# First loads of an attention and two-MoE kernel in another order, one weight tile decoded in halves

## The chip, the cores and the metric

The kernel runs on one core of a Trainium2 chip. The metric is device time in microseconds (us) of one execution; 1 us is 0.07% of it.

## The reference

Eight batches of eight heads attend, over 576 positions, to 32 memory slots that are built from the keys and values; two feed-forward layers follow. Cut to what matters:

```python
a = softmax(phi, axis=2)                                  # over the 32 slots
k_m, v_m = a^T @ k, a^T @ v                               # einsum bhsm,bhsd->bhmd
attn = softmax(q @ k_m^T / sqrt(64))
x = (attn @ v_m), heads side by side: [4608, 512]
x = (silu(x @ w_gate) * (x @ w_val)) @ w_out              # d_ff 1536
out = elu(x @ w_in) @ w_out2                              # d_ff 2048
```

The weights come as 64-bit floats, everything else as 32-bit.

## The kernel before

The heads' outputs are never formed. For each batch the 32 slots' values (vt, 128 partitions) are multiplied with the gate and value weights first, into vw (the product pvw, L237), and the softmaxed scores (at) are multiplied with vw (up1, L255 to L257). Each product that needs 32-bit accuracy is made of three fast ones: both sides are split into a high and a low part, and high x high, high x low and low x high are added.

The weights of the first layer lie in HBM as words of eight bytes. `words` and `load_w` (L119 to L144) decode a tile: one conversion on ScalarE (L126), then five steps on VectorE (L127, L128, L130, L131, L144). `load_wg(p, k2, pool, parts)` decodes tile k2 of pair p; pair p holds the weights for two of the hidden layer's blocks of 128 and comes as two tiles (k2 = 0, 1) of 1 MB. With `parts=2` a tile is decoded in two halves, ten steps of 128x512 for five of 128x1024. Tiles of pair 0 of the code are called **pair 1** here and in the change's description, those of `w1g[1, k2]` **pair 2**, with tile 0 (`raw[1, 0]`) and tile 1 (`raw[1, 1]`).

The stage around the change is the start (L506 to L534), for batch 0. ScalarE and VectorE softmax phi; TensorE transposes it (a_T, L347) and multiplies it with five chunks of keys and values (kv_mm, L364), the fifth of half size; the result is scaled (L371), transposed (L377) and copied to kT and vt (L380 to L388). Scores of the first half of the positions (L411) are transposed by VectorE (L416), reduced to a maximum (L422), subtracted (L423), passed through exp on ScalarE (L424), summed and divided (L429 to L432), and transposed back as ex (L451); ScalarE and VectorE split that into the high and low part of at (L453, L454). The second half's scores (L400, L402) go the same way in another layout. pvw of pair 1 (`vw(0, 0, G2)`) gives the first gate and value products; pvw of pair 2 comes inside the loop over batches, after a filler of 13 products that nobody reads (`spin`, L300). Copies of vw are ScalarE's L246 and L248, with a product by minus one (L247) between them. The output weights w1o are decoded there as well (`load_wo`; its split into woh is L171).

What sets the order: the loads are issued by SP in the order of the code. Each takes one of eight semaphores in turn, so a load is issued once the one eight before it has landed. The order of the instructions on TensorE, VectorE and ScalarE is made when the program is built, by a scheduler that starts what its own estimate of the times says is ready, `tc.high_priority()` first. On the chip each engine's list is fixed.

Of the kernel before, what the change touches and what calls it, by code (L numbers as in the profile page):

```python
# [27 lines left out]
NCH = 5  # L28
# [10 lines left out]
def attention_moe_moe(ctx: ExitStack, tc: tile.TileContext, qT, phiT, kv, kv4, w1g, w1o, w2, out):  # L39
# [5 lines left out]
    w1g, w1o, w2 = w1g.bitcast(I32), w1o.bitcast(I32), w2.bitcast(I32)  # L45

    dram = ctx.enter_context(tc.tile_pool(name="dram", bufs=1, space=DRAM))
    wa_p = ctx.enter_context(tc.tile_pool(name="wa", bufs=NWA))
# [53 lines left out]
    def fetch_part(r, src, i, parts=2):  # L102
        n = 1024 // parts
        cs = slice(n * i, n * i + n)
        nc.sync.dma_start(out=r[:, cs], in_=src[:, 2 * n * i:2 * n * i + 2 * n].rearrange("p (n t) -> p n t", t=2))
# [5 lines left out]
    def fetch_w(src):  # L111
        r = raw_tile()
        fetch_part(r, src, 0, 1)
        return r
# [26 lines left out]
    def load_w(v, r):  # L141
        with later():
            cf = words(v, r)
            last["sum"] = tt(out=v, in0=v, in1=cf, op=ALU.add)  # L144
# [4 lines left out]
    def load_wg(p, k2, pool, parts=1):  # L149
        t = pool.tile([128, 2, 512], F32, tag="w", name="wg")  # L150
        WG[p][2 * k2], WG[p][2 * k2 + 1] = t[:, 0], t[:, 1]
        r = raw.pop((p, k2), None)
        if r is None:
            r = fetch_w(w1g[p, k2])
        t = t.rearrange("p i c -> p (i c)")
        n = 1024 // parts
        for i in range(parts):
            cs = slice(n * i, n * i + n)
            load_w(t[:, cs], r[:, cs])
        ahead((p, k2))  # L160
# [30 lines left out]
    def ahead(key):  # L191
        if key in ORDER[:-1]:
            fetch_next(ORDER.index(key) + 1)
# [32 lines left out]
    raw = {}  # L226
# [248 lines left out]
    def back_tasks(b):  # L475
        z, nxt = Bs[b], Bs[b + 1] if 0 < b < B - 1 else None
        yield lambda: z.score(0)
        yield lambda: (z.norm(0), nxt and nxt.load_q(0))
        yield lambda: (z.attn(0))
        yield lambda: (z.score(1), 0 < b < B - 2 and Bs[b + 2].phi())  # L480
        yield lambda: (z.norm(1), nxt and nxt.load_q(1))
        yield lambda: (z.attn(1), z.store_at())
# [7 lines left out]
    def run(*gens):  # L490
        for g in gens:
            for t in g:
                t()
# [11 lines left out]
    z = Bs[0]  # L505
# [4 lines left out]
    z.load_kv(0)  # L510
    z.load_kv(1)
    fetch_part(raw[0, 1], w1g[0, 1], 0)
    for c in range(2, NCH):
        z.load_kv(c)
    fetch_part(raw[0, 1], w1g[0, 1], 1)
    z.load_q(0)
    for k2 in range(2):
        raw[1, k2] = vx_p.tile([128, 1024, 2], I32, tag="vx", name="wr1")
        fetch_part(raw[1, k2], w1g[1, k2], 0, 1)
        if k2 == 0:  # L520
            z.load_q(1)
    b0 = list(back_tasks(0))
    with tc.high_priority():
        z.phi()
# [3 lines left out]
    vw(0, 0, G2)  # L528
    first["ex"] = last["ex"]
    for k2 in range(2):  # L530
        load_wg(1, k2, wa_p)
    run(b0[3:])
    first["ex"] = last["ex"]
    load(Bs[1])  # L534
# [577 lines left out]
```

## Time and profile before

| | |
|---|---|
| median of 3 runs | 1433.72 us (1433.63 to 1433.94) |
| profiled execution, own time | 1434.55 us |
| its span in the trace | 1432.8 us |
| busy: TensorE, VectorE, ScalarE | 1405.6, 1141.7, 857.7 us |
| moved by DMA | 337.65 MB, mean 236 GB/s |
| mean granted clock of TensorE | 0.994 of full |

The span is what the trace covers; the execution's own time has 1.75 us around it. In the rows below a time is counted from the span's start. A duration of one instruction on VectorE or ScalarE overlaps the next one's start a little. A granted clock of 1.00 is 2.4 GHz, one of 0.50 is 1.2 GHz. SP's rows are issues of loads: the row is the issue, not the transfer.

### The profile page before, as it was taken

To read this page: it belongs to the slowest core of one execution; us is meant where nothing else is said; L and a number is where in the kernel's file an instruction comes from. 1 tells how busy PE (TensorE), PEld (TensorE's weight loads), DVE (VectorE), ACT (ScalarE), POOL (GpSimd) and SP (SyncE) were. 2 spreads that over 40 slices of the span, in tenths; PEclk is the share of its full clock that TensorE was granted. 3 is DMA by queue.
4 is the path that set the end of the run, shared out by engine and by line. 5 is a ranking of instruction groups with operands and counts; after the bars stand their busy time and mean duration, and the time that the engine had idled before them with its cause. 6 is when DMAs were issued, how large, how long until landed. Compare 5 with 4: busy or idle time off the path is not lost.

```text
span 1432.8 us, 23223 instructions
## 1 busy us (share of the span) xinstructions
PE 1405.6 (98%) x9269; PEld 1214.2 (85%) x9269; DVE 1141.7 (80%) x1462; ACT 857.7 (60%) x1251; POOL 44.8 (3%) x73
## 2 busy tenths in 40 slices
PE   6899999999999999999999999999999999999998
PEld 4688889998999999999998888888888888888887
DVE  7998887778798886886978578885898488957884
ACT  4665544544456465455656388556866588549843
POOL 0000000000000000000000000000000000000000
PEclk8999999999999999999999999999999999999999
DMA  9887512663789988888889866756675667666653
GB/s 375 321 315 283 195 74 101 224 226 140 265 246 291 297 237 255 258 243 270 282 272 364 282 198 213 273 205 197 205 275 210 199 205 254 224 206 204 214 199 131
DMA packets 89484, 337.65 MB, mean 236 GB/s; under 512 B 9376, under 2 KB 23712, under 8 KB 70048
## 3 DMA queue, kind: packets, MB, share of 16 engines
q1 hardware_dynamic: 55312, 254.04, 50.8%
q10 hardware_dynamic: 26880, 51.39, 9.7%
q0 software_dynamic: 7184, 30.74, 8.9%
q8 instruction: 73, 1.20, 0.3%
q14 instruction: 35, 0.29, 0.1%
HBM read 251.13 MB, written 85.00 MB: 235 GB/s over the span
## 4 chain that ended last, share of the span: by engine, by line
PE 90%; DVE 4%; DMA 3%; issue 1%; ACT 1%; SPq 0%; ACTq 0%; DVEq 0%
PE pu L834 12%; PE pu L832 12%; PE pu L833 12%; PE pd L834 5%; PE pd L832 5%; PE pd L833 5%; PE acc L262 4%; PE acc L260 4%; PE acc L261 4%; PE pv L255 3%; PE pg L255 3%; PE pv L257 3%; PE pv L256 3%; PE pg L257 3%; PE pg L256 3%; PE pvw L237 3%
## 5 line engine op out<-in xcount | busy, mean ns | idle before, releaser
L834 PE MATMUL pu<-xhi,w 128*128 128x512 f32 x672 | 261.4, 389 | 0.0
L833 PE MATMUL pu<-xlo,w 128*128 128x512 f32 x672 | 261.4, 389 | 0.0
L832 PE MATMUL pu<-xhi,w 128*128 128x512 f32 x672 | 261.4, 389 | 0.0
L861 ACT ACTIVATE xhi<-g 128x1024 fp32r<-128x1024 f32 x120 | 126.5, 1058 | 107.0 <-PE pu L834 64.5
L862 DVE TENSOR_TENSOR xlo<-g,xhi 128x1024 fp32r<-128x1024 f32 x120 | 145.3, 1223 | 40.7 <-ACT xhi L861 40.6
L833 PEld LDWEIGHTS pu<-xlo,w 128*128 128x128 f32 x672 | 126.1, 188 | 26.4
L834 PEld LDWEIGHTS pu<-xhi,w 128*128 128x128 f32 x672 | 126.1, 188 | 26.3
L832 PEld LDWEIGHTS pu<-xhi,w 128*128 128x128 f32 x672 | 126.1, 188 | 26.0
L261 PE MATMUL acc<-hh,ws 128*128 128x288 f32 x448 | 131.7, 296 | 0.0
L260 PE MATMUL acc<-hh,ws 128*128 128x288 f32 x448 | 131.5, 295 | 0.0
L262 PE MATMUL acc<-hl,ws 128*128 128x288 f32 x448 | 128.8, 297 | 0.0
L255 PE MATMUL pv<-at,vw 128*128 128x288 f32 x384 | 116.5, 303 | 1.9 <-DVE s L280 1.2
L255 PE MATMUL pg<-at,vw 128*128 128x288 f32 x384 | 116.7, 304 | 0.6 <-DVE gh L658 0.3
L722 ACT ACTIVATE hh<-gh 128x576 fp32r<-128x576 f32 x112 | 76.0, 685 | 67.8 <-PE acc L261 51.3
L256 PE MATMUL pg<-at,vw 128*128 128x288 f32 x384 | 114.0, 297 | 0.2 <-DVE at L454 0.2
L257 PE MATMUL pv<-at,vw 128*128 128x288 f32 x384 | 113.9, 297 | 0.0
L257 PE MATMUL pg<-at,vw 128*128 128x288 f32 x384 | 113.8, 297 | 0.1
L256 PE MATMUL pv<-at,vw 128*128 128x288 f32 x384 | 113.8, 296 | 0.0
L832 PE MATMUL pd<-xhi,w 128*128 128x512 f32 x288 | 112.0, 389 | 0.0
L833 PE MATMUL pd<-xlo,w 128*128 128x512 f32 x288 | 112.0, 389 | 0.0
L834 PE MATMUL pd<-xhi,w 128*128 128x512 f32 x288 | 112.0, 389 | 0.0
L852 DVE SCALAR_TENSOR_TENSOR et<-et 128x1024 f32<-128x1024 f32 x72 | 88.0, 1222 | 28.8 <-ACT et L851 28.8
(155 smaller groups left out, 3239.1 us busy)
## 6 DMA issues: line engine op xcount, KB each, us to landing
w<-dnd SPq DMA_DIRECT2D x64, 1024.0 KB, 4.9
w<-upd SPq DMA_DIRECT2D x40, 1024.0 KB, 5.6
w<-upd SPq DMA_DIRECT2D x32, 768.0 KB, 4.7
ws<-d1d SPq DMA_DIRECT2D x42, 512.0 KB, 5.1
kvr<-kv SPq DMA_DIRECT2D x32, 512.0 KB, 8.9
wr<-w SPq DMA_DIRECT2D x16, 1024.0 KB, 6.5
upd<-uw ACTq DMA_DIRECT2D x32, 512.0 KB, 7.1
dnd<-uw ACTq DMA_DIRECT2D x32, 512.0 KB, 8.2
```

Source lines behind the costliest of these rows:

```text
L255: mm(ps, lhsT=wh, rhs=ah, start=g == 0, stop=False)
L256: mm(ps, lhsT=wh, rhs=al, start=False, stop=False)
L257: last["pe"] = mm(ps, lhsT=wl, rhs=ah, start=False, stop=g == 1)
L260: mm(ps, lhsT=w[0][:, ms], rhs=hs[0], start=start, stop=False, skip_group_check=skip)
L261: mm(ps, lhsT=w[1][:, ms], rhs=hs[0], start=False, stop=False, skip_group_check=skip)
L262: mm(ps, lhsT=w[0][:, ms], rhs=hs[1], start=False, stop=stop, skip_group_check=skip)
L832: mm(ps, lhsT=w[0], rhs=x[0], start=start, stop=False, skip_group_check=skip)
L833: mm(ps, lhsT=w[0], rhs=x[1], start=False, stop=False, skip_group_check=skip)
L834: last["mm"] = mm(ps, lhsT=w[1], rhs=x[0], start=False, stop=stop, skip_group_check=skip)
L852: stt(out=a, in0=e, scalar=1.0, in1=a, op0=ALU.add, op1=ALU.mult)
L861: last["hi"] = act(out=hi, in_=x, func=AF.Copy)
L862: last["lo"] = tt(out=lo, in0=x, in1=hi.bitcast(F32), op=ALU.subtract)
```

## The change

Two edits. In the list of first loads, the second half of pair 1's tile 1 (its last quarter) goes ahead of key chunks 3 and 4; tile 0 of pair 2 is loaded in two halves, the first ahead of the first queries and the second between the first and second queries. And tile 0 of pair 2 is decoded in two halves (`load_wg(1, k2, wa_p, 2 - k2)`: two parts for k2 = 0, one for k2 = 1).

```diff
--- before.py
+++ after.py
@@ -510,15 +510,17 @@
     z.load_kv(0)
     z.load_kv(1)
     fetch_part(raw[0, 1], w1g[0, 1], 0)
-    for c in range(2, NCH):
-        z.load_kv(c)
+    z.load_kv(2)
     fetch_part(raw[0, 1], w1g[0, 1], 1)
-    z.load_q(0)
+    z.load_kv(3)
+    z.load_kv(4)
     for k2 in range(2):
         raw[1, k2] = vx_p.tile([128, 1024, 2], I32, tag="vx", name="wr1")
-        fetch_part(raw[1, k2], w1g[1, k2], 0, 1)
-        if k2 == 0:
-            z.load_q(1)
+    fetch_part(raw[1, 0], w1g[1, 0], 0)
+    z.load_q(0)
+    fetch_part(raw[1, 0], w1g[1, 0], 1)
+    z.load_q(1)
+    fetch_part(raw[1, 1], w1g[1, 1], 0, 1)
     b0 = list(back_tasks(0))
     with tc.high_priority():
         z.phi()
@@ -528,7 +530,7 @@
     vw(0, 0, G2)
     first["ex"] = last["ex"]
     for k2 in range(2):
-        load_wg(1, k2, wa_p)
+        load_wg(1, k2, wa_p, 2 - k2)
     run(b0[3:])
     first["ex"] = last["ex"]
     load(Bs[1])
```

The scheduler makes other lists from this. First place: around the first exp. In the names, wr_170 and wr_174 are the raw tiles 0 and 1 of pair 2 before; now they are wr_168 and wr_169. ScalarE before:

```order
L380 ACTIVATE kT<-ps_kvT 128x128
L386 ACTIVATE kTd<-ps_kvT 64x4x32 x2
L388 ACTIVATE vt<-ps_kvT 128x128
L126 ACTIVATE wg<-wr_170 128x1024
L424 ACTIVATE sc<-sc 128x576
L246 ACTIVATE vw<-pvw 128x512
L126 ACTIVATE wg<-wr_174 128x1024
L453 ACTIVATE at<-ex 128x2x288
L248 ACTIVATE vw<-pvw 128x512
```

ScalarE now:

```order
L126 ACTIVATE wg<-wr_168 128x512
L380 ACTIVATE kT<-ps_kvT 128x128
L386 ACTIVATE kTd<-ps_kvT 64x4x32 x2
L388 ACTIVATE vt<-ps_kvT 128x128
L126 ACTIVATE wg<-wr_168 128x512
L246 ACTIVATE vw<-pvw 128x512
L126 ACTIVATE wg<-wr_169 128x1024
L248 ACTIVATE vw<-pvw 128x512
L246 ACTIVATE vw<-pvw 128x512
L424 ACTIVATE sc<-sc 128x576
L248 ACTIVATE vw<-pvw 128x512
L453 ACTIVATE at<-ex 128x2x288
```

TensorE at the same place, as a piece of the difference:

```order
 L364 MATMUL ps_kvm<-kvr,a 32x128 x24
 L377 MATMUL ps_kvT<-ident,kvm 128x128 x2
+L237 MATMUL pvw<-wg,vt 32x512 x8
 L411 MATMUL ps_sc<-qr,kT 32x288 x8
-L237 MATMUL pvw<-wg,vt 32x512 x8
+L247 MATMUL pvw<-vw,minus 128x512
 L400 MATMUL ps_sc<-kTd,qr 128x2x32 x8
 L402 MATMUL ps_sc<-kTd,qr 32x64 x4
```

The first exp (L424 of sc) moved from right behind the conversion of tile 0 to behind the conversion of tile 1 and two copies of vw; the conversion of tile 0 is two rows. On TensorE pair 1's product pvw moved ahead of the first scores (L411).

Second place: VectorE around the end of pair 2's decoding (the last L144 of 128x1024), before:

```order
L144 TENSOR_TENSOR wg<-wg,wc 128x1024
L324 TENSOR_REDUCE nmx<-ph 128x2
L430 TENSOR_SCALAR smx<-smx 128x18
L287 SCALAR_TENSOR_TENSOR h<-s,pv 128x288
L268 TENSOR_TENSOR hl<-h,hh 128x288
L431 RECIPROCAL smx<-smx 128x18
L432 TENSOR_TENSOR sc<-sc,smx 128x576
L330 TENSOR_SCALAR rs<-sm 128x2
L331 RECIPROCAL rs<-rs 128x2
L268 TENSOR_TENSOR hl<-h,hh 128x288
L447 STREAM_TRANSPOSE ps_ex<-sc 128x32 x2
L127 TENSOR_SCALAR wc<-wv 128x1024
```

and now:

```order
L432 TENSOR_TENSOR sc<-sc,smx 128x576
L287 SCALAR_TENSOR_TENSOR h<-s,pv 128x288
L280 SCALAR_TENSOR_TENSOR s<-s,pg 128x288
L128 SCALAR_TENSOR_TENSOR wg<-wg,wc 128x1024
L287 SCALAR_TENSOR_TENSOR h<-s,pv 128x288
L268 TENSOR_TENSOR hl<-h,hh 128x288
L130 TENSOR_SCALAR wc<-wg 128x1024
L447 STREAM_TRANSPOSE ps_ex<-sc 128x32
L268 TENSOR_TENSOR hl<-h,hh 128x288
L131 SCALAR_TENSOR_TENSOR wc<-wr_169,wc 128x1024
L447 STREAM_TRANSPOSE ps_ex<-sc 128x32
L144 TENSOR_TENSOR wg<-wg,wc 128x1024
```

Eight steps that stood behind that last L144 now stand ahead of it: L430, L431 and L432 of the second softmax, one L287, two L268 and two L447 (L430 and L431 above the first row shown).

Third place: ScalarE around the copies of pair 2's vw (L246, L248), before:

```order
L266 ACTIVATE hh<-h 128x288
L246 ACTIVATE vw<-pvw 128x512
L348 ACTIVATE a<-ps_aT 128x512
L248 ACTIVATE vw<-pvw 128x512
L246 ACTIVATE vw<-pvw 128x512
L453 ACTIVATE at<-ps_ex 128x2x288
L348 ACTIVATE a<-ps_aT 128x512
L248 ACTIVATE vw<-pvw 128x512
L171 ACTIVATE woh<-wv 128x1024
```

and now:

```order
L327 ACTIVATE ph,sm<-ph,nmx 128x576 x2
L171 ACTIVATE woh<-wv 128x1024
L246 ACTIVATE vw<-pvw 128x512
L348 ACTIVATE a<-ps_aT 128x512
L248 ACTIVATE vw<-pvw 128x512
L246 ACTIVATE vw<-pvw 128x512
L126 ACTIVATE wv<-wr 128x1024
L348 ACTIVATE a<-ps_aT 128x512
L248 ACTIVATE vw<-pvw 128x512
```

The split of the output weights (L171) moved from behind the four copies to ahead of them, and the conversion of the second tile of output weights (L126 of wv) came in between.

## Rows read from the trace of the kernel before

**Rows 1.** The page, part 1: busy us (share of the span) and instructions of each engine
```profile
PE 1405.6 (98%) x9269; PEld 1214.2 (85%) x9269; DVE 1141.7 (80%) x1462; ACT 857.7 (60%) x1251; POOL 44.8 (3%) x73
```

**Rows 2.** Table of stretches, 27 to 43 us: busy us per engine, granted clock, DMA, GB/s
```profile
27.00:43.00 16.00, 12.18 (x62) 8.79 (x62) 15.93 (x25) 6.93 (x15) 0.00 (x0) 0.78 0.95 383
```

**Rows 3.** Timeline of SP, load issues: start us, us, engine, line, transfer, count
```profile
13.41 1.62 SPq L314 DMA_DIRECT2D kvr<-kv  x2
...
16.73 0.33 SPq L105 DMA_DIRECT2D wr<-w1o  x1
...
18.07 2.81 SPq L314 DMA_DIRECT2D kvr<-kv  x2
...
25.49 2.23 SPq L314 DMA_DIRECT2D kvr<-kv  x3
```

**Rows 4.** Timeline of TensorE, 15 to 23 us; in brackets the idle before and its releaser
```profile
15.19 2.26 PE L364 MATMUL ps_kvm<-kvr,a 128*32 128x128 f32 x48
...
19.05 0.72 PE L411 MATMUL ps_sc<-qr,kT 64*32 64x288 f32 x16 [0.37 <-ACT kT L380]
...
20.59 1.96 PE L237 MATMUL pvw<-wg,vt 64*32 64x512 f32 x16 [0.82 <-DVE wg L144]
```

**Rows 5.** Timeline of VectorE, 15 to 21 us: the last quarter of pair 1, first scores
```profile
15.22 0.69 DVE L144 TENSOR_TENSOR wg<-wg,wc 128x512 f32<-128x512 f32 x1
...
17.38 0.43 DVE L127 TENSOR_SCALAR wc<-wg 128x512 int32<-128x512 int32 x1 [1.47 <-ACT wg L126]
...
19.75 0.69 DVE L144 TENSOR_TENSOR wg<-wg,wc 128x512 f32<-128x512 f32 x1
...
20.36 0.84 DVE L416 STREAM_TRANSPOSE sc<-ps_sc 128x288 f32<-128x288 f32 x2
```

**Rows 6.** Timeline of ScalarE, 19 to 27 us: vt, exp, copy of vw, tile 1
```profile
19.45 0.28 ACT L388 ACTIVATE vt<-ps_kvT 128x128 f32<-128x128 f32 x1
...
22.82 0.68 ACT L424 ACTIVATE sc<-sc 128x576 f32<-128x576 f32 x1 [1.15 <-DVE sc L423]
...
23.40 0.58 ACT L246 ACTIVATE vw<-pvw 128x512 fp32r<-128x512 f32 x1
...
25.45 1.15 ACT L126 ACTIVATE wg<-wr 128x1024 f32<-128x1024 f32 x1 [1.47 <-DMA wr<-w1g]
```

**Rows 7.** Timeline of VectorE, 25 to 47 us
```profile
25.62 0.78 DVE L451 STREAM_TRANSPOSE ex<-sc 128x576 f32<-128x576 f32 x1
...
26.32 1.25 DVE L127 TENSOR_SCALAR wc<-wg 128x1024 int32<-128x1024 int32 x2
...
38.12 1.22 DVE L144 TENSOR_TENSOR wg<-wg,wc 128x1024 f32<-128x1024 f32 x1
...
39.26 1.35 DVE L324 TENSOR_REDUCE nmx<-ph 128x2 f32<-128x1152 f32 x1
...
40.52 0.17 DVE L430 TENSOR_SCALAR smx<-smx 128x18 f32<-128x18 f32 x1
...
43.39 0.49 DVE L447 STREAM_TRANSPOSE ps_ex<-sc 128x32 f32<-128x32 f32 x2 [0.25 <-PE ps_ex L444]
...
45.64 0.75 DVE L454 TENSOR_TENSOR at<-ps_ex,at 128x576 fp32r<-128x576 f32 x1
```

**Rows 8.** Timeline of TensorE, 39 to 56 us
```profile
39.49 1.09 PE L237 MATMUL pvw<-wg,vt 64*32 64x512 f32 x16 [0.83 <-DVE wg L144]
...
43.18 0.50 PE L247 MATMUL pvw<-vw,minus 128*128 128x512 f32 x1
...
47.79 2.41 PE L364 MATMUL ps_kvm<-kvr,a 64*32 64x128 f32 x80 [0.63 <-ACT a L342]
...
55.63 0.33 PE L347 MATMUL ps_aT<-ident,ph 128*128 128x128 f32 x1 [1.19 <-ACT ph L327]
```

**Rows 9.** Table of stretches, 54 to 60 us
```profile
54.00:57.00 3.00, 1.38 (x22) 0.75 (x7) 3.00 (x6) 2.29 (x5) 0.00 (x0) 1.00 1.02 406
...
57.00:60.00 3.00, 2.78 (x15) 2.54 (x14) 3.00 (x9) 3.00 (x6) 0.00 (x0) 0.64 1.02 414
```

## The prediction

> **What bounds the kernel now.** I read the busy times first: TensorE works 98% of the span [rows 1], so a change to the first loads can only pay, or cost, where TensorE still waits. The table of stretches puts that at the start: between 27 and 43 us it works 12.18 of 16 us, and some of that is a filler that computes nothing (spin), while VectorE works 15.93 of 16 [rows 2]. In that stretch VectorE's list is the bound. Before it, the DMA queue is: its issue rows are the list of landings, because each load waits for the one eight before it. Keys chunk 2 landed at 13.41, chunk 3 at 13.41 + 1.62 - 0.33 = 14.70, the last quarter of pair 1 at 16.73, the first queries at 18.07, tile 0 of pair 2 at 20.55, its tile 1 at 25.49 [rows 3]. So 512 KB take 1.3 us and the DMA engines are full. No order of the loads makes tile 1 earlier: the same bytes stand ahead of it.
>
> About 0.2% (2.9 us) is what a measurement of this kernel can tell from no change.
>
> **Part 1: the loads.** One quarter (512 KB) goes ahead of 768 KB of keys. By 1.3 us for 512 KB it lands at 14.7, keys 3 and 4 at 16.0 and 16.7, the half tile at 18.0, the first queries at 19.4, the second half at 20.7, the second queries at 22.0, tile 1 still at 25.5. One more DMA is issued: 0.33 us on SP, which waits for landings anyway, so nothing. The later keys cost nothing either: their products run from 15.19 to 17.45 in three equal parts [rows 4], so chunk 4 is wanted only at about 16.7. That cover has no slack: if the keys land later, the whole chain moves by as much (0 to 0.4 us; I take 0).
>
> **Part 2: the gain.** The last quarter of pair 1 is decoded on VectorE from 17.38 to 20.44 [rows 5], 3.06 us. It can now start when the quarter before is done, 15.22 + 0.69 = 15.9, and ends at 19.0. Its product pvw then waits for vt, ready at 19.45 + 0.28 = 19.73 [rows 6]: it starts at 19.8 and not at 20.59 [rows 4]. Gain: 0.8 us.
>
> **Part 3: the scores go behind it.** TensorE's list now has pvw ahead of the first scores. pvw takes 1.96, the scores 0.72 [rows 4]: they end at 22.4, before at 19.77. VectorE took them at 20.36 [rows 5] and now at 22.45, 2.1 later. From there to the exp were 2.46 us (22.82 less 20.36) [rows 5, 6], so its operand is ready at 24.9.
>
> **Part 4: the exp goes behind a load.** This is the term that decides. In ScalarE's list the first exp stood ahead of the conversion of tile 1, and now stands behind it and behind two copies of vw. That conversion started at 25.45, when its DMA landed, and took 1.15; a copy takes 0.58 [rows 6]. Starts follow each other some 0.08 before an end, so the exp starts at 25.5 + 1.15 + 2 x 0.58 - 0.25 = 27.55, not at 22.82. VectorE, whose list goes on only with that exp, idles from 24.9 to 28.2.
>
> The six landings above came in the order of issue [rows 3]. The Trainium skill (DMA: Bandwidth & Descriptors, Queues, rings and completion order) says that completion is not first-in first-out per issuing engine. If by that rule tile 1 came by 22.6, the exp would start at 24.9, and the sum below would be 9.1 instead of 11.8; no row here shows such an overtaking.
>
> **Part 5: to the first gate product.** From exp to the end of the transpose ex took 25.62 + 0.78 - 22.82 = 3.58 [rows 6, 7]. One operation of 0.7 (the maximum of the second half, as long as the 0.75 of L454, less overlap [rows 7]) now stands in between. ex ends at 31.8, before at 26.4: 5.4 late.
>
> **Part 6: VectorE's list to the end of pair 2.** From 26.32 to 39.34 it needed 13.0 us without a gap [rows 2, 7]. Decoding tile 0 in halves makes five operations ten: 2 x (2 x 0.43 + 3 x 0.69) = 5.86 [rows 5] for 2 x 0.63 + 3 x 1.22 = 4.92 [rows 7], less 0.08 of overlap for each of the five more: +0.5. The list now also takes, ahead of the last sum of pair 2, eight steps that stood behind it: from 40.52 to 43.88, less 0.25 of idle and 0.3 for two small steps that stay behind: +2.8. The maximum went ahead: -0.7. That is 15.6, so pair 2 is decoded at 47.4, and its pvw starts then and not at 39.49 [rows 8]: 7.9 late. In the old trace TensorE had waited 0.83 us for it [rows 8]; its work ahead of pvw is 5.4 late and pvw 7.9, so it waits some 3.3 us here.
>
> **Part 7: the copies of vw.** ScalarE's list has the split of the output weights, woh (L171), ahead of the first copy. It needs four VectorE steps that stand behind pair 2: L324 1.35, L454 0.75, L127 0.63, L128 1.22 [rows 7], 3.65 with overlaps, so 51.05. Then woh, by the 1024-wide conversion's 1.15, and the copy, 0.58 [rows 6]: TensorE's L247 starts at 52.7 instead of 43.18 [rows 8], 9.6 late. The last copy of vw stands behind the conversion of the second output tile (L126), which waits for four more VectorE steps, 0.63 and 3 x 1.22 less overlaps: 55.05. Conversion 1.15, two copies of 0.6: 57.2, where before the products of keys could begin at 47.79 [rows 8] after the same tail of some 1.5. They now begin at 58.7: **10.9 late**.
>
> **Part 8: what comes after.** From there TensorE's work is the same and bounds the stage, so a delay stays unless later waits shrink. Those before: 1.19 us ahead of 55.63 [rows 8] and a fall of the granted clock to 0.64 in 57 to 60 us, where 3 us times 0.36 is 1.1 us [rows 9]. By bounds: all of it saved is -2.3, and up to 4 more if the clock stays at its lower level through the new gaps. In the old trace a stretch with TensorE busy 1.38 of 3 us was followed by that fall [rows 9], and the new order has such gaps ahead of the first gate product (to 32.6), of pair 2's pvw (to 47) and of L247 (to 52.7), so I take +0.9, near one such fall.
>
> **Sum.** 10.9 + 0.9 = 11.8, the gain of 0.8 being already in it (Part 3 starts from it). On the profiled execution, 1434.55 us (span 1432.8), that is 1446.4; on the median of the runs, 0.8 lower at 1433.72, it is **1445.5**.
>
> **Rivals.**
> A, not slower. VectorE has empty time in the new order, 19.0 to 22.4 and 24.9 to 28.2, and the halves of tile 0 (5.4 us of decoding, in memory at 18.0 and 20.7) fit in it. If they ran there, tile 0 would be done before the exp, pair 2 would be ready 5 us sooner in the list, and with the exp not held up the wait of 0.83 ahead of pvw [rows 8] would go: 1433.72 - 0.8 - 0.8 = 1432.1, and at best another 1.2 for a wait shortened behind it: 1431. It decides whether L127 of tile 0 runs ahead of the transpose ex. For it: the data is there in time. Against it: VectorE's list has L127 behind ex, and no row here shows an engine leaving its list. 0.05. The Trainium skill (Perfetto Trace Analysis, Optimizing Scalar/DVE Operations) says that where these engines are not saturated but cause bubbles, breaking up instructions may let work end sooner; by that rule this rival would win.
>
> B, no change: hidden anyway. TensorE is busy 98%, and the delay is absorbed by its later waits. Those shown are 1.19 and the fall of 1.1 us; they would have to be 8 us more: 1433.7 to 1436.6. 0.05.
>
> C, slower, but less: the rows' extra microsecond ahead of tile 1's landing (1024 and 576 KB in 4.9 us behind tile 0, for 3.9 by the pace above [rows 3]) does not come again, and the later waits go. 10.9 - 1.0 - 2.3 = 7.6, or 1441.3; with one of Part 7's waits shorter by 1.2, 1440. This is inside my range.
>
> D, slower by more: the clock stays low from 33 to 60 us and every product in the gaps takes double: +4, and more waits in the orders behind. 1450 and above. 0.10.
>
> **How the numbers follow.** Forecast with C: 0.80; A 0.05, of which faster by over 0.2% needs 2.9 us, more than its 2.7, so 0.02; B 0.05; D 0.10. Faster 0.02, same 0.08, slower 0.90. The range takes C's 1440 as its low end and D's beginning, 1450, as its high end: it leaves out A, B and most of D, 0.2.
>
> **What would show it.** Right: ScalarE's conversion of the 128x1024 tile waiting for its DMA until 24.4 to 25.5 and the exp right behind the two copies, at about 27.5; VectorE idle for some 3 us before its sum over that exp; TensorE idle around 30; pair 2's pvw near 47; the products of keys for the next batch near 58.7. Wrong: the exp at 23 to 25 us, or pvw before 41.

## The result, and the profile after

The changed kernel took **1448.28 us** in the median of four runs (1447.47 to 1449.07), the kernel before 1433.83 beside it: ratio 1.0097, 95% interval 1.0084 to 1.0109. It is slower by 14.5 us. The profiled execution took 1447.73 us, 13.2 more than that of before (1434.55); its span is 1446.0 instead of 1432.8 [rows 1].

The page, first part:

```profile
span 1446.0 us, 23234 instructions
...
PE 1405.1 (97%) x9269; PEld 1214.7 (84%) x9269; DVE 1144.1 (79%) x1467; ACT 859.3 (59%) x1252; POOL 44.8 (3%) x73
```

TensorE is as busy in sum as before (1405.6), with the same number of instructions, so the whole difference is time in which it waits. Where that is, the table of stretches says; its columns are the stretch, its length, busy time and instructions of TensorE, of its weight loads, of VectorE, ScalarE and GpSimd, the granted clock, the DMA engines' share and GB/s. Before, from 0 to 200 us:

```profile
0.00:50.00 50.00, 33.01 (x315) 23.53 (x315) 40.87 (x68) 24.61 (x48) 0.99 (x8) 0.86 0.87 340
50.00:100.00 50.00, 47.26 (x559) 37.16 (x553) 48.70 (x96) 33.05 (x73) 0.00 (x0) 0.97 0.94 352
100.00:150.00 50.00, 49.46 (x557) 42.46 (x556) 42.23 (x85) 27.98 (x65) 0.00 (x0) 1.00 0.72 254
150.00:200.00 50.00, 50.00 (x559) 42.87 (x558) 41.08 (x80) 26.25 (x62) 0.00 (x0) 1.00 0.45 157
```

The changed kernel:

```profile
0.00:50.00 50.00, 26.47 (x209) 18.41 (x210) 36.49 (x66) 20.48 (x39) 0.99 (x8) 0.81 0.82 325
50.00:100.00 50.00, 43.71 (x560) 35.47 (x558) 44.29 (x80) 31.48 (x67) 0.00 (x0) 0.95 0.89 306
100.00:150.00 50.00, 48.38 (x572) 39.86 (x565) 45.37 (x91) 28.52 (x70) 0.00 (x0) 1.00 0.78 262
150.00:200.00 50.00, 47.73 (x470) 41.55 (x469) 37.37 (x73) 25.33 (x58) 0.00 (x0) 1.00 0.52 180
```

TensorE works 6.5, 3.6, 1.1 and 2.3 us less in these four stretches, 13.4 together: all of the difference lies in the first 200 us, and three quarters of it in the first 100. What TensorE waits for, in the timeline (start, duration, engine, line, operation, tiles; in brackets the idle time before and what ended it):

```profile
15.40 2.46 PE L364 MATMUL ps_kvm<-kvr,a 128*32 128x128 f32 x48
...
20.21 1.22 PE L237 MATMUL pvw<-wg,vt 64*32 64x512 f32 x16 [1.09 <-ACT vt L388]
21.12 1.26 PE L411 MATMUL ps_sc<-qr,kT 64*32 64x288 f32 x16
...
32.54 0.61 PE L255 MATMUL pg<-at,vw 128*128 128x288 f32 x1 [3.93 <-ACT at L453]
...
46.72 1.09 PE L237 MATMUL pvw<-wg,vt 64*32 64x512 f32 x16 [3.54 <-DVE wg L144]
...
51.99 0.79 PE L247 MATMUL pvw<-vw,minus 128*128 128x512 f32 x1 [1.49 <-ACT vw L246]
...
59.41 2.41 PE L364 MATMUL ps_kvm<-kvr,a 64*32 64x128 f32 x80 [1.71 <-ACT a L342]
...
157.96 0.40 PE L260 MATMUL pd<-hh,woh 128*128 128x288 f32 x1 [2.15 <-ACT p L544]
```

Pair 2's weight products stood at 39.49, L247 at 43.18 and the products of the next keys at 47.79 [rows 8]: they are 7.2, 8.8 and 11.6 us late. ScalarE shows why, in its timeline:

```profile
19.88 0.28 ACT L388 ACTIVATE vt<-ps_kvT 128x128 f32<-128x128 f32 x1
...
25.66 1.12 ACT L126 ACTIVATE wg<-wr 128x1024 f32<-128x1024 f32 x1 [3.59 <-DMA wr<-w1g]
26.69 0.58 ACT L248 ACTIVATE vw<-pvw 128x512 fp32r<-128x512 f32 x1
27.16 0.59 ACT L246 ACTIVATE vw<-pvw 128x512 fp32r<-128x512 f32 x1
27.64 0.69 ACT L424 ACTIVATE sc<-sc 128x576 f32<-128x576 f32 x1
...
50.40 1.06 ACT L171 ACTIVATE woh<-wv 128x1024 fp32r<-128x1024 f32 x1 [0.85 <-DVE wv L128]
51.36 0.58 ACT L246 ACTIVATE vw<-pvw 128x512 fp32r<-128x512 f32 x1
...
57.76 1.13 ACT L126 ACTIVATE wg<-wr 128x1024 f32<-128x1024 f32 x1 [0.89 <-DMA wr<-w1g]
```

The first exp (L424) is at 27.64 instead of 22.82 [rows 6]. ScalarE stood idle for 3.59 us ahead of the conversion of tile 1, which waits for its load and stands in front of the exp. The exp's operand was ready at 24.20 + 0.76 = 24.96 (L423 below), so the exp lost 2.7 us behind that conversion and two copies; the other 2.1 us or so are the scores', which now stand behind pvw on TensorE. VectorE, in its timeline, idles 3.40 us for that exp; its transpose ex comes at 31.00 instead of 25.62 and pair 2's last sum at 45.35 instead of 38.12 [rows 7]:

```profile
22.53 0.85 DVE L416 STREAM_TRANSPOSE sc<-ps_sc 128x288 f32<-128x288 f32 x2 [3.69 <-PE ps_sc L411]
...
24.20 0.76 DVE L423 TENSOR_TENSOR sc<-sc,mx 128x576 f32<-128x576 f32 x1
28.36 0.75 DVE L429 TENSOR_REDUCE smx<-sc 128x18 f32<-128x576 f32 x1 [3.40 <-ACT sc L424]
...
31.00 0.77 DVE L451 STREAM_TRANSPOSE ex<-sc 128x576 f32<-128x576 f32 x1
...
45.35 1.22 DVE L144 TENSOR_TENSOR wg<-wg,wc 128x1024 f32<-128x1024 f32 x1
```

SP's issue rows, which are the landings, came as the change sets them (each row waits for the load eight places ahead): 14.66 for the last quarter, 16.61 the last keys, 17.96 the half tile, 19.32 the first queries (18.07 before [rows 3]), and tile 1 last, just ahead of 25.66:

```profile
14.66 1.61 SPq L314 DMA_DIRECT2D kvr<-kv  x2
16.61 0.33 SPq L318 DMA_DIRECT2D qr<-qT  x1
17.96 0.33 SPq L105 DMA_DIRECT2D wr<-w1o  x1
19.32 1.59 SPq L314 DMA_DIRECT2D kvr<-kv  x2
```

### The profile page after: what moved, and what is told of

Same layout as the page of the kernel before. It is cut to its first block, busy times and chain, and to the rows that moved or that the text cites. A ratio compares the mean times of both kernels' runs of the same rounds, so it can differ in the third digit from the quotient of the medians.

```text
span 1446.0 us, 23234 instructions
## 1 busy us (share of the span) xinstructions
PE 1405.1 (97%) x9269; PEld 1214.7 (84%) x9269; DVE 1144.1 (79%) x1467; ACT 859.3 (59%) x1252; POOL 44.8 (3%) x73
## 4 chain that ended last, share of the span: by engine, by line
PE 85%; DVE 5%; DMA 2%; issue 1%; ACT 1%; ACTq 0%; DVEq 0%; SPq 0%
PE pu L834 12%; PE pu L835 12%; PE pu L836 12%; PE pd L834 5%; PE pd L835 5%; PE pd L836 5%; PE acc L262 4%; PE acc L260 4%; PE acc L261 4%; PE pg L255 3%; PE pv L255 3%; PE pv L257 3%; PE pv L256 3%; PE pg L257 3%; PE pg L256 3%; PE pvw L237 2%
```

## The experiments

A change in the order of loads does two things at once. The bytes arrive in another order; and, since the order of every engine's instructions is fixed when the kernel is built, from modelled times, the engines get other lists too. **Theory 1** is that the lists make the loss: in three pieces up to 50 us (the exp behind a conversion that waits for a load; more VectorE steps ahead of pair 2's last sum; woh ahead of pair 2's copies) and a rest behind. **The rivals** are that the loads' order makes it, that the halving makes it, and that the exp's wait alone makes it.

All runs, times in us; exp, pvw of pair 2 and the next keys' products are starts in the profiled execution. The kernel before ran beside each group, with medians of 1433.86 to 1434.46.

| Run | Median | Ratio, 95% interval | exp | pvw | next keys |
|---|---|---|---|---|---|
| before | 1433.83 | 1 | 22.82 | 39.49 | 47.79 |
| changed | 1448.28 | 1.0084 to 1.0109 | 27.64 | 46.72 | 59.41 |
| changed, exp first | 1442.97 | 1.0053 to 1.0076 | 23.53 | 42.82 | 55.19 |
| changed, tile 0 whole | 1442.29 | 1.0041 to 1.0065 | 28.07 | 44.82 | 54.12 |
| before, tile 0 in halves | 1438.64 | 1.0026 to 1.0050 | 22.79 | 41.76 | 53.35 |
| half tile moved alone | 1444.99 | 1.0060 to 1.0084 | 22.91 | 42.67 | 52.56 |
| last quarter moved alone | 1440.06 | 1.0029 to 1.0054 | 22.24 | 39.98 | 49.40 |
| changed, scores first | 1443.57 | 1.0055 to 1.0083 | 22.62 | 42.39 | 52.26 |
| scores first, tile 0 whole | 1440.79 | 1.0034 to 1.0060 | 22.55 | 42.21 | 49.04 |
| exp first, woh last | 1447.19 | 1.0075 to 1.0103 | 24.58 | 44.30 | 56.66 |
| loads only | 1434.44 | 0.9989 to 1.0007 | 23.00 | 39.68 | 47.98 |
| order only | 1445.80 | 1.0061 to 1.0086 | 26.42 | 45.50 | 58.23 |
| before, wait only | 1437.88 | 1.0014 to 1.0032 | 26.57 | 43.23 | 51.52 |
| changed, again | 1447.24 | 1.0077 to 1.0105 | 27.48 | 46.56 | 59.09 |

### The exp ahead of tile 1's conversion

```
-            act(out=sc, in_=sc, func=AF.Exp, ...)
+            last["exp"] = act(out=sc, in_=sc, func=AF.Exp, ...)
...
-        load_wg(1, k2, wa_p, 2 - k2)
+        with tc.issue_after(last["exp"].ins) if k2 else nullcontext():
+            load_wg(1, k2, wa_p, 2 - k2)
```

> The changed kernel, with one pin: the conversion of pair 2's tile 1 (which waits for its load until 25.7) stands behind the first exp on ScalarE; the order of every other engine is the changed kernel's. Theory 1 (the order that the change brought about costs the time, in three pieces: the exp behind that conversion, the longer list of VectorE steps ahead of pair 2's last sum, woh ahead of pair 2's copies): the exp's input is there at 24.96 (24.20 + 0.76 in the changed kernel's trace), so the exp starts at 25.0 instead of 27.64; the first gate product starts near 30 (32.54), pair 2's weight products near 44.1 (46.72), the products of the next keys near 56.8 (59.41). About 2.6 us come back, no more, since the other two pieces stay: 1445.7 (1444.7 to 1446.7). Rival: the exp's place makes the whole loss, then 1434 to 1437. Rival: the loads' order makes the loss (keys and queries later) and the exp's place is only where it shows: 1447.5 to 1449.

Measured: 1442.97, 5.3 under the changed kernel in its first runs and 4.3 under it when it ran again (below). In the timelines of ScalarE and TensorE:

```profile
23.53 0.68 ACT L424 ACTIVATE sc<-sc 128x576 f32<-128x576 f32 x1 [0.34 <-DVE sc L423]
25.33 1.13 ACT L126 ACTIVATE wg<-wr 128x1024 f32<-128x1024 f32 x1 [1.12 <-DMA wr<-w1g]
...
42.82 1.96 PE L237 MATMUL pvw<-wg,vt 64*32 64x512 f32 x16 [3.13 <-DVE wg L144]
...
55.19 2.41 PE L364 MATMUL ps_kvm<-kvr,a 64*32 64x128 f32 x80 [1.17 <-ACT a L342]
```

The pin moves one row of ScalarE's list, the conversion, behind the two copies and the exp. The exp is 4.1 us earlier and the next keys' products 4.2. The direction is Theory 1's; the size I had too small, because the exp's input came at 23.5 and not at 24.96. When the changed kernel ran again, that input was ready at 23.73 and the exp started at 27.48: there the wait behind the conversion is 3.75 us, not 2.7. The scores took 0.69 us here and 1.26 in the changed kernel's trace: the granted clock was 1.00 from 18 to 24 us here, and 0.51 from 21 to 24 there. 8.7 us of loss stay with the exp back in its place, so its wait is not all of it.

### Halves or whole

Two runs take the halving apart from the loads. First the changed kernel's loads with tile 0 decoded whole:

```
-        load_wg(1, k2, wa_p, 2 - k2)
+        load_wg(1, k2, wa_p)
```

> The changed kernel's loads, tile 0 of pair 2 decoded whole (one conversion and four VectorE steps of 128x1024 instead of two sets of 128x512). By its order the exp is still behind tile 1's conversion, so it stays near 27.6 and ex near 31.0. Theory 1: between ex and pair 2's last sum VectorE has steps that add up to about 14.1 us instead of 15.6 by the durations of before's and the changed kernel's rows, and woh stands behind the first three copies of pair 2 instead of ahead of the first; so pair 2's weight products near 45 and the products of the next keys near 54.5 to 55 instead of 59.41: 3 to 5 us come back, 1443 to 1446. Rival (the halving makes the loss): 1433 to 1436. Rival (the loads' order makes it, decoding has no part): 1447.5 to 1449.

Measured: 1442.29, 0.7 under the range expected; the exp still waits (28.07), the next keys' products come at 54.12, near the 54.5 to 55 expected. Then before's loads with the halves:

```
-        load_wg(1, k2, wa_p)
+        load_wg(1, k2, wa_p, 2 - k2)
```

> Before's loads in before's order, tile 0 of pair 2 decoded in halves. By its order the exp stays ahead of tile 1's conversion, so the first exp is near 22.8 and the first gate product near 27.2 as before. Theory 1: the halves alone bring the longer list ahead of pair 2's last sum (tile 1's steps stand behind the second softmax instead of between tile 0's), so pair 2's weight products come near 42 (before 38.87), and the products of the next keys near 52 (47.79): 1437 to 1440, a loss without any load moved and without the exp's wait. Rival (the exp's wait makes all of the loss): 1433 to 1435. Rival (the loads' order makes it): 1433 to 1435.

Measured: 1438.64, as Theory 1 has it. No load moved and the exp at 22.79, and still 4.4 us slower: with tile 0 in halves, tile 1's steps stand behind the second softmax on VectorE, and pair 2 is ready 2.3 us later. TensorE in the timeline:

```profile
41.76 1.09 PE L237 MATMUL pvw<-wg,vt 64*32 64x512 f32 x16 [0.73 <-DVE wg L144]
```

So the halving, with the lists that come of it, is a second piece, and neither piece is the whole.

### Half a tile alone, the last quarter alone, and the scores first

Half a tile of pair 2 ahead of the first queries, the last quarter left where it was (against before; the lines that these replace are left out):

```
+    fetch_part(raw[1, 0], w1g[1, 0], 0)
     z.load_q(0)
+    fetch_part(raw[1, 0], w1g[1, 0], 1)
+    z.load_q(1)
+    fetch_part(raw[1, 1], w1g[1, 1], 0, 1)
...
-        load_wg(1, k2, wa_p)
+        load_wg(1, k2, wa_p, 2 - k2)
```

> Only half a tile of pair 2 ahead of the first queries, with that tile decoded in halves; the last quarter of pair 1 stays behind the keys as before. By its order the scores are again ahead of pair 1's weight products and the exp ahead of tile 1's conversion. Theory 1: the queries land about 1.3 later than before's 18.07, the exp near 23.2 instead of 22.8, the first gate product near 27.6; the longer VectorE list stays, pair 2's weight products near 42 to 42.5, the products of the next keys near 52 to 53: 1438 to 1441, some 8 to 10 us under the changed kernel, which then belong to the last quarter's move (it turns scores and weight products round and puts the exp behind the wait). Rival (the later queries and keys make the loss): 1445 to 1449. Rival (the exp's wait makes all of the loss): 1433 to 1435.

Measured: 1444.99, 4 us above the upper end of the expectation. Up to the next keys' products all is as said (22.91, 42.67, 52.56); the rest, some 6 of the 10.8 us between the profiled spans (1443.6 and 1432.8), is lost behind, where this theory had nothing. Then the last quarter alone:

```
-    for c in range(2, NCH):
-        z.load_kv(c)
+    z.load_kv(2)
     fetch_part(raw[0, 1], w1g[0, 1], 1)
+    z.load_kv(3)
+    z.load_kv(4)
```

> Only the last quarter of pair 1 moved ahead of keys 3 and 4; the rest of before's loads and the whole decode kept. By its order TensorE's first 36 groups are before's; ScalarE and VectorE differ in a few neighbours from 23 us on (woh two steps earlier, one s and one h step exchanged with pair 2's last sums). Theory 1 (what counts is the order of the engines, and a load that comes earlier than its consumer needs it gives nothing): keys 3 and 4 land about 1.3 later, which costs 0.2 to 0.4 as in the changed kernel; pair 1's weight products wait for vt as before and gain nothing; pair 2's copies and the products of the next keys come up to 1.3 later: 1434 to 1438. Rival (the loads' order itself makes the loss, the last quarter's above all, as the half tile alone gave 1445 of 1448): 1437 to 1441, with the clock and the first products late. Rival (the earlier decode is a gain): under 1433.

Measured: 1440.06, where up to 1438 was expected, and inside the range of the rival that blames the loads. Its exp is at 22.24, ahead of before's, and the next keys' products are only 1.6 late. Of the 5.7 us between the profiled spans (1438.5 and 1432.8) 4.1 are lost later. TensorE's list is before's up to those products; ScalarE's parts a little earlier (+ this kernel, against before, as built):

```
 L246 ACTIVATE vw<-pvw 128x512
 L453 ACTIVATE at<-ps_ex 128x2x288
+L171 ACTIVATE woh<-wv 128x1024
 L348 ACTIVATE a<-ps_aT 128x512
 L248 ACTIVATE vw<-pvw 128x512
```

woh now stands ahead of pair 2's last copies, and TensorE waits 1.61 us for the last copy, which it did not wait for in before. Further on, a product of the output projection waits 2.36 us for an eviction:

```profile
48.33 0.41 PE L257 MATMUL pg<-at,vw 128*128 128x288 f32 x1 [1.61 <-ACT vw L248]
...
150.94 0.40 PE L260 MATMUL pd<-hh,woh 128*128 128x288 f32 x1 [2.36 <-ACT p L543]
```

The changed kernel has the same wait of 2.15 at 157.96. Next, the changed kernel with pair 1's weight products pinned behind the first scores, as in before:

```
-                return mm(ps[g][32 * j:32 * j + 32], lhsT=self.kT[r, j, :], ...)
+                last["sc"] = mm(ps[g][32 * j:32 * j + 32], lhsT=self.kT[r, j, :], ...)
+                return last["sc"]
...
-    vw(0, 0, G2)
+    with tc.issue_after(last["sc"].ins):
+        vw(0, 0, G2)
```

> The changed kernel's loads and halves, with one pin: pair 1's weight products stand behind the first scores on TensorE, as before. All engines then have the order of the kernel with the half tile alone moved (but for one exchange of two ScalarE steps at 15 us), so the first exp is ahead of tile 1's conversion again; only the last quarter's load is elsewhere. Theory 1 (the order decides): the same time as that kernel, 1443.5 to 1446, some 3 under the changed kernel, although the exp starts near 23 instead of 27.6. Rival (the scores' and the exp's place make most of the loss): 1434 to 1438. Rival (the loads' order): 1447.5 to 1449.

Measured: 1443.57, as expected. Its operations come in the order of the kernel with the half tile alone (1444.99) on all three engines to the end, but for one exchange of two ScalarE steps at 15 us; only one load has another place, and the intervals overlap. The same pin with tile 0 decoded whole leaves of the change only its loads and what the lists became:

```
-        load_wg(1, k2, wa_p, 2 - k2)
+        load_wg(1, k2, wa_p)
...
-    vw(0, 0, G2)
+    with tc.issue_after(last["sc"].ins):
+        vw(0, 0, G2)
```

> The changed kernel's loads alone: tile 0 decoded whole, and pair 1's weight products pinned behind the first scores. The order of all engines is then before's up to 24 us, and close to before's up to 50 (woh one copy earlier, the two last sums of pair 2 next to each other, the transposes of ex behind those of the next keys). Theory 1: the first exp near 23, the first gate product near 27.6, pair 2's weight products 41 to 42.5, the products of the next keys 49 to 51 (before 47.79, changed kernel 59.41): 1435 to 1440. Rival (the loads' order in itself): 1445 to 1449. Rival (no loss left at all, loads and the later order cost nothing): 1433 to 1434.6.

Measured: 1440.79, 0.8 over Theory 1's range. The exp (22.55) and the next keys' products (49.04) are near before's, and 6.9 us are lost all the same. By now every kernel whose lists were built anew had lost 4 us or more, and the loads' order could still be to blame.

### woh behind the copies

```
-            wo = [lambda u=u: load_wo(u, wo_p) for u in range(UA // 2)]
+            wo = [lambda: None] * 3 + [lambda u=u: load_wo(u, wo_p) for u in range(UA // 2)]
...
-            act(out=hi, in_=v, func=AF.Copy)
+            with tc.issue_after(last["cp"].ins):
+                act(out=hi, in_=v, func=AF.Copy)
```

with the exp's pin from above; `last["cp"]` is the last copy of vw (L248), and lines move by one.

> The changed kernel with two pins: the exp ahead of tile 1's conversion (as in the run that gave 1442.97), and woh, whose load and decode are issued three turns later, behind pair 2's four copies on ScalarE, as in before. Theory 1: the wait of TensorE for the first of those copies (1.5 us, ScalarE waiting 0.85 for wv and then 1.06 in woh) goes away, pair 2's copies come some 1.8 us earlier (45.7 instead of 47.46), and the products of the next keys come 0.3 to 2 us earlier, since ScalarE's conversion of the next pair's tile now stands ahead of the second wv: 1439 to 1442. Rival (woh's place costs nothing, the wait is made up behind it): 1442.5 to 1443.5. Rival (the clock: what comes back is lost to a later fall): 1443.5 to 1446.

Measured: 1447.19, and the expectation fell, the third piece's with it. The wait of 1.5 ahead of L247 did go. But the conversion of pair 3's tile stands ahead of the last copy of the transposed features (L342, here L343), as in the changed kernel, and its load now landed at 55.30, 1.8 us later than with the exp's pin alone (53.53). TensorE waits 3.33 us for that copy (1.17 there), and the products behind it take 4.27 us instead of 2.41, at the lower clock. ScalarE and TensorE in the timeline:

```profile
55.30 1.14 ACT L126 ACTIVATE wg<-wr 128x1024 f32<-128x1024 f32 x1 [1.55 <-DMA wr<-w1g]
56.34 0.26 ACT L343 ACTIVATE a<-ps_aT 128x128 f32<-128x128 f32 x1
...
56.66 4.27 PE L365 MATMUL ps_kvm<-kvr,a 64*32 64x128 f32 x80 [3.33 <-ACT a L343]
```

It is the pattern of the first exp once more: a ready step behind one that waits for a load. But this execution does not show woh's place alone. Its exp is at 24.58 and its pvw at 44.30, 1.05 and 1.48 us later than with the exp's pin alone, and its granted clock was 0.50 from 21 to 24 us where that was 1.00; most of the 1.8 us may come from there. Its time, 1449.73, is the longest of five (from 1443.48). So the median says that this pin gained nothing; what woh's place costs stays open.

### Loads and lists taken apart

The next two runs exchange one for the other. The loads' issues on SP are put into another order after the lists of all engines are fixed; each issue keeps its own waits and signals. **Loads only**: before's lists, with tile 0 fetched in two halves (which leaves the first 2000 rows of each engine as they were), and the changed kernel's order on SP. **Order only**: the changed kernel's lists, and before's order on SP. In the traces the operations of TensorE, VectorE and ScalarE come in before's order to the end in the first, and in the changed kernel's order in the second. Some issues are later than in the kernel whose loads they copy, since their waits stay (the last quarter at 6.87 us in loads only, at 4.62 in the changed kernel).

```
+    for blk in nc.main_func.blocks:
+        sp = [i for i, x in enumerate(blk.instructions) if x.opcode == "DMACopy" and str(x.engine).endswith("SP")]
+        if len(sp) > 20:
+            at, order = sp[6:6 + 9], [0, 3, 1, 2, 5, 4, 6, 7, 8]
+            old = [blk.instructions[i] for i in at]
+            for i, n in zip(at, order):
+                blk.instructions[i] = old[n]
+            break
     r = run_bass_kernel_spmd(nc, [arrays], core_ids=[0])
```

(loads only; order only has `[0, 2, 3, 1, 5, 4, 6, 7, 8]`.)

> The changed kernel's loads, in its order and sizes, under the order that PE, ScalarE and VectorE have in the kernel before: tile 0 of pair 2 is fetched in two halves but decoded whole, and the issues on SP are exchanged only after the order of the engines has been set; the first 2000 rows of each of the three engines are before's. Theory 1 (the loss is the order that was rebuilt around the new loads): before's time within 1 us, 1433.4 to 1435.2, with the first exp near 23, pair 2's weight products 39 to 40 and the products of the next keys 47.5 to 48.5; keys 3 and 4 cost at most 0.4. Rival (the loads' order in itself): 1437 to 1441, as the kernel with the last quarter alone (1440.06) and the one with all loads moved and the scores first (1440.79) would then show. Rival (a gain is there that the order hides): under 1432.5.

Measured: 1434.44 beside 1434.41, ratio 0.9998, interval 0.9989 to 1.0007. The timelines of ScalarE and TensorE:

```profile
19.24 1.22 PE L411 MATMUL ps_sc<-qr,kT 64*32 64x288 f32 x16 [0.99 <-DMA qr<-qT]
...
23.00 0.68 ACT L424 ACTIVATE sc<-sc 128x576 f32<-128x576 f32 x1 [1.43 <-DVE sc L423]
...
39.68 1.09 PE L237 MATMUL pvw<-wg,vt 64*32 64x512 f32 x16 [0.87 <-DVE wg L144]
...
47.98 2.41 PE L364 MATMUL ps_kvm<-kvr,a 64*32 64x128 f32 x80 [0.62 <-ACT a L342]
```

The scores wait 0.99 us for the later queries; the exp and the next keys' products are 0.2 late, and that is all that the new order of loads costs up to there; the medians do not differ.

> The other half of the exchange: the order of the changed kernel on PE, ScalarE and VectorE and its halves, but the issues on SP put back in before's order (keys 3 and 4 ahead of the last quarter, the first queries ahead of tile 0's first half, whose two halves then follow each other), after the order of the engines was set. Theory 1: the exp still waits behind tile 1's conversion (tile 1 lands at the same place in the queue, 25.4 to 25.7), so nothing of the loss goes: 1446.5 to 1449. The last quarter, 1.3 later, delays pair 1's weight products and the scores behind them by up to 1 us, in the shade of the exp's wait. Rival (the loads' order in itself makes a part of the loss): 1440 to 1445.

Measured: 1445.80, 0.7 under the expectation and 0.8 over the rival's range, ratio 1.0074 (1.0061 to 1.0086):

```profile
24.41 1.14 ACT L126 ACTIVATE wg<-wr 128x1024 f32<-128x1024 f32 x1 [0.85 <-DMA wr<-w1g]
...
26.42 0.68 ACT L424 ACTIVATE sc<-sc 128x576 f32<-128x576 f32 x1
...
58.23 2.41 PE L364 MATMUL ps_kvm<-kvr,a 64*32 64x128 f32 x80 [1.74 <-ACT a L342]
```

Tile 1 landed 1.25 us earlier here than in the changed kernel's trace (24.41, not 25.66), and the exp and the next keys' products moved with it, by 1.22 and 1.18. Such a landing is not tied to before's order of loads: with the changed order, tile 1's conversion started at 24.29 in the kernel with the scores first and tile 0 whole, and at 24.25 in loads only. So the lists carry a loss of 11.4 us with before's loads too, and the loads carry none with before's lists.

### The wait put into the kernel before, and the changed kernel again

In before's lists the conversion of tile 0 stands right ahead of the first exp. With tile 1 and the second queries issued ahead of tile 0, that conversion gets the late load:

```
+            at, order = sp[6:6 + 8], [0, 1, 2, 3, 4, 7, 6, 5]
```

> The kernel before with the suspected wait put into it and nothing else: the order of PE, ScalarE and VectorE is before's, only two loads are exchanged on SP after that order was set, tile 1 of pair 2 ahead of the second queries and tile 0 behind them. ScalarE's conversion of tile 0, which stands just ahead of the first exp in before, then waits for the last load (24.4 to 25.5) instead of the one before it, so the first exp starts at 25.5 to 26.7 instead of 22.8, nearly as late as in the changed kernel (27.64); ex, the first gate product and the VectorE steps behind them come as much later. Theory 1 (the exp's wait is one piece of the loss and passes on at its full size; the longer VectorE list, woh and the order up to 200 us are the rest): 2.7 to 3.8 us, 1436.5 to 1439. Rival (the exp's wait makes nearly all of the changed kernel's loss): 1444 to 1449. Rival (it is swallowed by the spin products and the waits behind them): 1433.5 to 1435.

Measured: 1437.88, ratio 1.0023 (1.0014 to 1.0032), as Theory 1 has it:

```profile
25.55 1.12 ACT L126 ACTIVATE wg<-wr 128x1024 f32<-128x1024 f32 x1 [6.23 <-DMA wr<-w1g]
26.57 0.67 ACT L424 ACTIVATE sc<-sc 128x576 f32<-128x576 f32 x1
...
43.23 1.09 PE L237 MATMUL pvw<-wg,vt 64*32 64x512 f32 x16 [0.86 <-DVE wg L144]
...
51.52 2.41 PE L364 MATMUL ps_kvm<-kvr,a 64*32 64x128 f32 x80 [0.63 <-ACT a L342]
```

The exp is 3.75 us late, pvw 3.74, the next keys' products 3.73: on this stretch the wait passes on whole, and the median is 3.4 up.

> The changed kernel as it is, beside the runs of this study, to set it against the kernel with its order and before's loads (1445.8). Theory 1 (the loads cost nothing; that kernel's advantage is the last load's landing, 24.4 against 25.66 in the changed kernel's trace, and no effect of the order of loads): 1445 to 1449, with tile 1's landing and the first exp moving together. Rival (its loads cost it 2.5 us more than before's loads do under the same order): 1447.5 to 1449, with tile 1's landing at 24.4 and the exp at 26.4.

Measured: 1447.24, and tile 1's conversion at 25.51 with the exp at 27.48. The interval (1.0077 to 1.0105) overlaps that of the order alone, so a cost of the loads under the changed lists is not shown. The medians differ by 1.4 us; in the traces the exp is 1.06 and the next keys' products 0.86 earlier with the order alone, as tile 1's landing is (1.10), so the landing can make up most of it. The intervals are too wide to say that the loads cost nothing here.

No run beat the kernel before: the changed loads under before's lists equal it.

## Why the prediction was right

The forecast was 1445.5, in 1440 to 1450, slower with 0.90. It came out 2.8 us too low, inside the range, by the mechanism it named up to the next keys' products; behind them (Part 8) the cause was another.

- **Part 1, loads.** The landings came at 14.66, 16.61, 17.96 and 19.32, where 14.7, 16.7, 18.0 and 19.4 were forecast, and tile 1 last. The later keys were taken at 0 with up to 0.4 as the bound: their products ended at 15.40 + 2.46 = 17.86, not 17.45 [rows 4]: 0.4 late. The rule of the Trainium skill that was weighed there (DMA: Bandwidth & Descriptors, Queues, rings and completion order), that completion is not first-in first-out, had no effect here: tile 1, issued last, was there last (25.66). What shows it is ScalarE's wait for it; SP's rows, from which the prediction read the order of landing, could not show an overtaking, since each of them comes behind the one before.
- **Parts 2 and 3.** pvw came at 20.21 (19.8), held by the keys' 0.4; VectorE took the scores at 22.53 (22.45). That is in part luck: pvw was put at 1.96 and the scores at 0.72, and they took 1.22 and 1.26, since the granted clock fell between them; when the changed kernel ran again, VectorE took the scores at 21.30. The exp was hardly touched by it (27.48), because it waits for tile 1.
- **Part 4, the term that decides.** The exp came at 27.64 (27.55), VectorE idled 3.40 us (3.3). The runs show the wait as a cause: 3.4 us where it was put into before, 4.3 to 5.3 where it was taken out of the changed kernel. But "decides" says too much: by the sum's own terms it was less than half of 11.8, and so it is.
- **Part 5.** ex ended at 31.00 + 0.77 = 31.77 (31.8).
- **Part 6, VectorE's list.** From 31.69, where L127 starts, to the end of pair 2's last sum at 45.35 + 1.22 = 46.57 it needed 14.9 us, not 15.6: this term was 0.7 too large. Most of that is in the eight steps, which move the list on by 2.2 us here, counted from start to start, and not by 2.8. TensorE's wait was 3.54 (3.3). The halves alone under before's loads cost 4.4 us, by this list and what follows from it.
- **Part 7, woh and the copies.** L247 came at 51.99 (52.7), 0.7 early from Part 6. The next keys' products came at 59.41 (58.7), 0.7 late: a step was missing in the working. The last copy ended at 56.29 + 0.58 = 56.87 (57.2), but from there it took 2.5 us and not 1.5, because ScalarE's conversion of pair 3's tile stands ahead of L342, and waited 0.89 us for its load until 57.76.
- **Part 8, what comes after: +0.9, too small and by the wrong cause.** The profiled execution lost 13.2 - 11.6 = 1.6 us there. The prediction put it down to a fall of the clock. The clock did fall, to 0.50 to 0.80 between 48 and 57 us, but that is ahead of the next keys' products and so inside Part 7. Behind them it stands at 1.00; it is before that was lower there, 0.91 from 47.8 to 60 us and 0.90 from 60 to 66. What grew are the waits. The table of stretches, from the next keys' products on, before and then the changed kernel:

```profile
47.80:200.00 152.20, 148.92 (x1743) 124.42 (x1744) 134.21 (x262) 87.52 (x201) 0.00 (x0) 0.99 0.71 256
59.40:211.60 152.20, 145.52 (x1719) 122.03 (x1720) 130.49 (x254) 84.98 (x198) 0.00 (x0) 1.00 0.70 242
```

TensorE idles 3.28 us in the one and 6.68 in the other, 3.4 more, of which the higher clock gave back some 1.7 (an estimate: 12.2 x 0.09 + 6 x 0.10). One of these waits is the 2.15 us at 157.96, and the kernel with the last quarter moved lost 4.1 us behind the next keys' products. The prediction had read the new lists only up to 60 us, and the ones behind are new as well. So 0.7 of the 2.8 us comes from Part 7 and 0.7 from Part 8; the other 1.4 is that the median of the changed kernel is 0.55 above its profiled run, while before's is 0.83 below its own.
- **Rival A** needed VectorE to take tile 0's halves in its empty time. It idled 3.69 and 3.40 us with that data in memory (the second half from 20.6 on), in front of steps that were not ready: the list is kept, and the halves alone cost 4.4 us. The rule of the Trainium skill (Perfetto Trace Analysis, Optimizing Scalar/DVE Operations) that breaking up instructions may let work end sooner is said of engines that are not saturated. VectorE, at 15.93 of 16 us where these steps run [rows 2], is saturated there, so this cost does not contradict the rule.
- **Rival C**'s earlier landing came in the run with the order alone, and some 1.2 us of the loss went with it in the trace; B and D did not come.

What stays open: which exchange in the lists from 60 to 200 us costs how much. It was seen as waits in two kernels, not undone one by one, since a pin moved other steps too (woh behind the copies). Nor is it shown that the pieces add: the exp's wait (3.4 to 5.3 us) and the halves (4.4) leave 3 us or more of the 12.8 to 14.5.

## What to carry to other kernels

When loads are moved in a kernel whose instruction order is built from modelled times, read the new lists of every engine before the landings: look for a step that is ready behind one that waits for a load, on the engine that everything else waits for. To know whether the data's order or the instructions' order makes a difference, exchange the issues on the load queue after the lists are fixed, so that one changes and the other does not. A small edit can cost more through the lists far behind it (for one load moved by two places, 4.1 of 5.7 us were lost behind 49 us) than at its own place.

## What was not expected of the hardware

- **When the clock falls first.** With nearly the same work up to 21 us, the granted clock stood at 0.51 from 21 to 24 us in the changed kernel's trace and at 1.00 in that of the same kernel run again, where it fell to 0.80 from 24 to 27. The scores' 16 products took 1.26 us in the one and 0.69 in the run with the exp first. It moved the exp's operand by more than a microsecond; whether it is also why the runs of one kernel spread (1441.58 to 1447.99 with the exp first) was not tried.
- **When the last load lands.** Tile 1, behind the same bytes, was converted from 24.29 (scores first, tile 0 whole), 24.41 (order only), 25.51 and 25.66 (the changed kernel twice) and 26.09 (tile 0 whole) on, where ScalarE waited for nothing else. The first and the last of these have the same order of loads. What makes the difference was not tried.
